# Decode attention on one core: one head of four batches a step, 8 KB of keys per partition, Q used as transposed

## The chip, the cores and the metric

One core of a Trainium2 chip. The metric is the device time of one execution, in microseconds (us). Each run has a state: "fast", or "slow" where it lies over 1.5% above the fastest of the same kernel, and "unknown" where there is only one.

Engine names in the profile: PE is the matmul engine, PEld its weight load, DVE the vector engine, ACT the scalar engine, POOL the general-purpose engine, SP the engine that issues the DMAs (SPq is its queue). L848 means line 848 of that kernel's source. Line numbers shift between kernels.

## The reference

Two attention layers, A and B, whose outputs are joined along the last axis. Both have 16 batches, 32 query tokens a batch, a model width of 1024, 32 query heads of 128 and 1024 cached keys. A has 4 key/value heads, each used by 8 query heads; B has 32, one per query head. All data is bf16.

```python
q = transpose((x @ wq).reshape(B, Sq, H, Dh), 0, 2, 1, 3)
scores = einsum("bhqd,bhkd->bhqk", q, k_cache) * (Dh ** -0.5)
p = softmax(scores, axis=-1)
o = einsum("bhqk,bhkd->bhqd", p, v_cache)
return transpose(o, 0, 2, 1, 3).reshape(B, Sq, H * Dh) @ wo
```

B's key cache has 16 x 32 heads of 256 KB (1024 keys x 256 bytes): 134 MB. B's values are as much again, and everything together is 340 MB. Neighbouring heads of one batch lie next to each other in memory; the same head of the next batch lies 32 heads, 8 MiB, further on.

## The kernel before

The kernel is a list of operations with declared reads and writes, ordered by a list scheduler. B runs in 128 steps. A step handles four (batch, head) pairs of 32 queries, so that the 128 rows of a score tile are full. The four pairs are two neighbouring heads of two batches.

Keys arrive with the key index on the partitions. Four 32-partition quadrants of the PE array are used as separate small arrays (32x32 tiles, 402 ns a score matmul); a DVE transpose (on pairs of bf16, 1223 ns for 128x1024 of them) puts the head dimension on the 32 partitions of a quadrant.

```python
# B's step: heads h0, h0+1 of batches b0, b0+1
ksrc = pb["k"][q.b0:q.b0 + 2, q.h0:q.h0 + 2].rearrange("t hh (p s) d -> (hh p) t (s d)", s=16)
pr.add("sp", lambda e: e.dma_start(KB_sb[:, sl, :, :], ksrc), ...)            # 1 MB, two pieces of 4 KB a partition
for t_ in range(2):
    vsrc = pb["v"][q.b0 + t_, q.h0:q.h0 + 2].rearrange("hh (p c) d -> p hh c d", c=NCH)
    pr.add("sp", lambda e, ...: e.dma_start(VB_sb[:, sl, t_, :, :, :], vsrc), ...)   # 512 KB, 2 KB pieces
# ... (cut)
# transposes of the keys, two a step
pr.add("dve", lambda e: e.transpose(KBt_sb[:, sl, t_, :].bitcast(F32), KB_sb[:, rs, t_, :].bitcast(F32)), ...)
```

A head's keys fill 64 partitions, two quadrants, so the queries of one batch are needed in all four quadrants. After the transpose of the projected queries (`QBt`) they lie in one quadrant only. Small matmuls with an identity, the "shuffle", copy them, and ACT moves the result to `QR`:

```python
for rg in range(4):
    last = e.matmul(QSH[0][32 * rg:32 * rg + 32, 0:2 * Dh]..., ident[32 * a:32 * a + 32, 32 * a:32 * a + 32], rhs,
                    start=True, stop=True, tile_position=(32 * a, 32 * rg))
# ... (cut)
evac(QR[:, gp, a, :, :], QSH[0][:, 0:2 * Dh]..., eng="act", ...)
```

The rest of a step: scores into PSUM, one exp over 128x1024 (1029 ns) with the row sum as a by-product (200 ns for its read), a PE transpose of the probabilities, their product with V, and the scaling. A's steps, projections and output products are put between by the scheduler. Two key slots and three value slots are the buffers.

## Time and profile before

| | before |
|---|---|
| time, median of 3 runs | 914.93 us (910.07 to 921.08) |
| the one issuing queue, share of 16 DMA engines | 97.6% |
| PE busy | 783.4 us, 86% |
| DVE, ACT busy | 57%, 51% |

The first lines come from the page of the kernel before: busy time per engine as a share of the span, then one digit per fortieth of the span (the busy tenths of the 16 DMA engines), then the packets that the DMA engines moved, counted cumulatively by size, and the queue's share of the 16 engines' time.

```profile
span 911.5 us, 28186 instructions
...
PE 783.4 (86%) x12610; PEld 432.9 (47%) x12610; DVE 519.3 (57%) x891; ACT 462.1 (51%) x853; POOL 67.9 (7%) x76
...
DMA  9789899999999999999999999999999999899995
...
DMA packets 151934, 341.64 MB, mean 375 GB/s; under 512 B 10496, under 2 KB 26880, under 8 KB 151808
q1 hardware_dynamic: 151808, 339.78, 97.6%
```

The DMA engines have almost no free time in any slice; PE is next. The following line is from the table by stretches (window, length, busy us and count for PE, PEld, DVE, ACT and POOL, then granted PE clock, DMA share, GB/s). In the middle of the kernel the share is a little over 1, because packets overlap somewhat (17 or more were in flight during 385 us of the span, my own count).

```profile
300.00:323.00 23.00, 20.13 (x354) 10.64 (x341) 12.53 (x22) 10.26 (x21) 2.08 (x2) 0.93 1.04 409
```

Three groups of the kernel before, with busy us, mean ns of one, and idle time ahead of them with what ended it: the key transpose; the shuffle (split by shape, since its tile is shared with other matmuls) and the ACT copies behind it.

```profile
L848 DVE STREAM_TRANSPOSE KBt_sb<-KB_sb 128x1024 f32<-128x1024 f32 x256 | 306.6, 1223 | 46.3 <-DMA KB_sb<-in_B_k_cache_dram 22.6
...
L694 PE MATMUL ps_pj<-QBt,ident 32*32 32x256 bf16 x512 | 43.9, 287 | 17.5 <-ACT QR L588 10.0 <-DVE acc L748 2.6 <-DVE Qtok L590 1.5
...
L588 ACT CAST QR<-ps_pj 128x256 bf16<-128x256 f32 x128 | 48.5, 379 | 46.0 <-PE ps_pj L694 43.3
```

The transposes wait only 22.6 us in all for the key DMA. Last, the DMA issues (count, KB each, us from issue to landing):

```profile
KB_sb<-in_B_k_cache_dram SPq DMA_DIRECT2D x128, 1024.0 KB, 8.2
VB_sb<-in_B_v_cache_dram SPq DMA_DIRECT2D x256, 512.0 KB, 8.9
```

The single packet records of the trace give the price of a packet on one engine. This is my own count, not a view of the profile:

```
before: size   packets   mean ns   median ns
1 KB           16384      49.4      46
2 KB           92160      85.2      84
4 KB           32768     167.3     159        (all of B's keys)
8 KB              32     351.7     309        (instruction fetches)
```

### The profile page before, as it was taken

To read this page: it belongs to the slowest core of one execution; us is meant where nothing else is said; L and a number is where in the kernel's file an instruction comes from. 1 tells how busy PE (TensorE), PEld (TensorE's weight loads), DVE (VectorE), ACT (ScalarE), POOL (GpSimd) and SP (SyncE) were. 2 spreads that over 40 slices of the span, in tenths; PEclk is the share of its full clock that TensorE was granted. 3 is DMA by queue.
4 is the path that set the end of the run, shared out by engine and by line. 5 is a ranking of instruction groups with operands and counts; after the bars stand their busy time and mean duration, and the time that the engine had idled before them with its cause. 6 is when DMAs were issued, how large, how long until landed. Compare 5 with 4: busy or idle time off the path is not lost.

```text
span 911.5 us, 28186 instructions
## 1 busy us (share of the span) xinstructions
PE 783.4 (86%) x12610; PEld 432.9 (47%) x12610; DVE 519.3 (57%) x891; ACT 462.1 (51%) x853; POOL 67.9 (7%) x76
## 2 busy tenths in 40 slices
PE   5879999999998899988898789989897888978775
PEld 2325564545554454545454455536453445545332
DVE  1415655466645566555756556666665656666553
ACT  2215665655564455655564555555554544646242
POOL 0000000100110010101010010001010100001000
PEclk7879999999999999999999999999999899989898
DMA  9789899999999999999999999999999999899995
GB/s 333 270 302 370 308 399 361 402 385 390 359 380 409 411 349 400 401 381 392 368 405 403 411 374 390 375 346 397 405 408 399 385 398 403 333 409 397 385 410 190
DMA packets 151934, 341.64 MB, mean 375 GB/s; under 512 B 10496, under 2 KB 26880, under 8 KB 151808
## 3 DMA queue, kind: packets, MB, share of 16 engines
q1 hardware_dynamic: 151808, 339.78, 97.6%
q8 instruction: 101, 1.65, 0.7%
q14 instruction: 25, 0.20, 0.1%
HBM read 337.64 MB, written 2.10 MB: 373 GB/s over the span
## 4 chain that ended last, share of the span: by engine, by line
PE 56%; ACT 14%; DVE 13%; DMA 12%; issue 2%; SPq 2%; POOL 0%; POOLq 0%; DVEq 0%; ACTq 0%
PE ps_pj L735 10%; PE ps_s L887 10%; DVE KBt_sb L848 6%; PE ps_o L971 6%; PE ps_pj L657 6%; PE ps_pt L921 6%; ACT P_sb L907 5%; PE ps_pj L674 5%; PE ps_kt L937 4%; DMA KB_sb<-in_B_k_cache_dram 4%; ACT PTA_sb L901 3%; PE ps_s L865 3%; DMA wq_sb<-in_A_wq_dram 3%; DVE acc L748 3%; PE ps_kt L839 2%
## 5 line engine op out<-in xcount | busy, mean ns | idle before, releaser
L848 DVE STREAM_TRANSPOSE KBt_sb<-KB_sb 128x1024 f32<-128x1024 f32 x256 | 306.6, 1223 | 46.3 <-DMA KB_sb<-in_B_k_cache_dram 22.6
L887 PE MATMUL ps_s<-KBt_sb,QR 32*32 32x512 bf16 x4096 | 167.0, 402 | 13.8 <-ACT P_sb L907 7.4
L901 ACT ACTIVATE PTA_sb<-ps_s 128x1024 bf16<-128x1024 f32 x128 | 131.6, 1029 | 73.1 <-PE ps_s L865 59.9
L907 ACT ACTIVATE P_sb<-ps_s 128x1024 bf16<-128x1024 f32 x128 | 131.7, 1029 | 70.3 <-PE ps_pt L921 36.5
L588 ACT COPY PT_sb<-ps_pt 128x512 f32<-128x512 f32 x128 | 74.9, 585 | 150.6 <-PE ps_o L971 116.5
L822 POOL COPY VAp_sb<-VA_sb 128x1024 bf16<-128x1024 bf16 x64 | 66.6, 1040 | 770.5 <-DMA VA_sb<-in_A_v_cache_dram 667.3
L921 PE MATMUL ps_pt<-id,P_sb 128*128 128x128 f32 x512 | 91.7, 302 | 18.4 <-ACT P_sb L907 16.9
L987 DVE TENSOR_SCALAR OB_sb<-ps_o,rinv_all 128x128 bf16<-128x128 f32 x128 | 44.4, 347 | 108.0 <-PE ps_o L971 107.6
L921 PEld LDWEIGHTS ps_pt<-id,P_sb 128*128 128x128 f32 x512 | 74.2, 208 | 43.2 <-ACT P_sb L907 25.2
L971 PE MATMUL ps_o<-VB_sb,PT_sb 128*32 128x128 bf16 x4096 | 84.9, 224 | 8.4 <-DMA VB_sb<-in_B_v_cache_dram 6.7
L865 PE MATMUL ps_s<-QT_sb,KTA_sb 128*128 128x256 bf16 x512 | 85.3, 275 | 4.2 <-ACT PTA_sb L901 2.2
L735 PE MATMUL ps_pj<-woB_sb,OTB_sb 128*128 128x512 bf16 x256 | 75.4, 391 | 12.9 <-DVE acc L748 5.4
L937 PE MATMUL ps_kt<-VAp_sb,PTA_sb 128*128 128x129 bf16 x1024 | 80.3, 221 | 5.4 <-ACT KTA_sb L588 2.3
L971 PEld LDWEIGHTS ps_o<-VB_sb,PT_sb 128*32 128x32 bf16 x4096 | 60.1, 98 | 52.1 <-issue 38.7
L657 PE MATMUL ps_pj<-xT_sb,wq_sb 128*128 128x512 bf16 x256 | 74.0, 406 | 11.4 <-DMA wq_sb<-in_A_wq_dram 4.2
L887 PEld LDWEIGHTS ps_s<-KBt_sb,QR 32*32 32x32 bf16 x4096 | 49.7, 90 | 67.5 <-issue 19.5
L937 PEld LDWEIGHTS ps_kt<-VAp_sb,PTA_sb 128*128 128x128 bf16 x1024 | 64.9, 98 | 31.2 <-issue 13.4
L674 PE MATMUL ps_pj<-wq_sb,xT_sb 128*128 128x512 bf16 x256 | 71.0, 391 | 4.3 <-ACT QR L588 1.8
L735 PE MATMUL ps_pj<-woA_sb,OTA_sb 128*128 128x512 bf16 x256 | 66.9, 389 | 7.4 <-DVE ost L751 4.7
L588 ACT CAST QR<-ps_pj 128x256 bf16<-128x256 f32 x128 | 48.5, 379 | 46.0 <-PE ps_pj L694 43.3
L748 DVE TENSOR_TENSOR acc<-acc,ps_pj 128x512 f32<-128x512 f32 x64 | 43.5, 680 | 44.6 <-PE ps_pj L735 44.2
L865 PEld LDWEIGHTS ps_s<-QT_sb,KTA_sb 128*128 128x128 bf16 x512 | 44.3, 98 | 32.3 <-ACT PTA_sb L901 5.8
(52 smaller groups left out, 574.0 us busy)
## 6 DMA issues: line engine op xcount, KB each, us to landing
KB_sb<-in_B_k_cache_dram SPq DMA_DIRECT2D x128, 1024.0 KB, 8.2
VB_sb<-in_B_v_cache_dram SPq DMA_DIRECT2D x256, 512.0 KB, 8.9
KA_sb<-in_A_k_cache_dram SPq DMA_DIRECT2D x64, 256.0 KB, 9.5
VA_sb<-in_A_v_cache_dram SPq DMA_DIRECT2D x64, 256.0 KB, 7.7
wq_sb<-in_B_wq_dram SPq DMA_DIRECT2D x32, 256.0 KB, 6.9
wq_sb<-in_A_wq_dram SPq DMA_DIRECT2D x32, 256.0 KB, 8.7
woB_sb<-in_B_wo_dram SPq DMA_DIRECT2D x32, 256.0 KB, 8.4
woA_sb<-in_A_wo_dram SPq DMA_DIRECT2D x32, 256.0 KB, 7.8
```

Source lines behind the costliest of these rows:

```text
L588: pr.add("act", lambda e: e.copy(dst_ap, src_ap), reads=reads, writes=writes, name=name + "@act", wtag=wtag, rtag=rtag)
L657: last = e.matmul(ps_pj[:, 0:tn], wq_sb[:, 0, j, hc * Dh:(hc + 1) * Dh], xT_sb[:, 0, j, t0:t0 + tn], start=(j == 0), stop=(j == DJ - 1))
L674: last = e.matmul(ps_pj[:, 0:CW], xT_sb[:, 1, j, G * P:(G + 1) * P], wq_sb[:, 1, j, :], start=(j == 0), stop=(j == DJ - 1))
L735: last = e.matmul(ps_pj[:, 0:OUTW], OT[:, gp, hh, :], wo_[:, hh, oh * OUTW:(oh + 1) * OUTW], start=(hh == 0), stop=(hh == nh - 1))
L848: pr.add("dve", lambda e: e.transpose(KBt_sb[:, sl, t_, :].bitcast(F32), KB_sb[:, rs, t_, :].bitcast(F32)), reads=[("KB", rs)], writes=[(" ...
L865: last = e.matmul(ps_s[:, sbf, c2, i * 2 * P:(i + 1) * 2 * P], KTA_sb[:, sl, c * P:(c + 1) * P], qt, start=True, stop=True)
L887: last = e.matmul(ps_s[32 * cg:32 * cg + 32, sbf, g2, :].rearrange("p (s j) -> p s j", s=16), lhsT, rhs, start=(fp == 0), stop=(fp == 3), ...
L901: pr.add("act", lambda e: e.activation(dst, src, ACTF.Exp, scale=scale), writes=BK_S[sbf] + [("PTA", q.half)], name="expA", rtag={("Sv", s ...
L907: pr.add("act", lambda e: e.activation(dst, src, ACTF.Exp, scale=scale, accum_out=stat[:, 0:1]), writes=BK_S[sbf] + ["P", "rowsum"], name= ...
L921: last = e.transpose(ps_pt32[:, m * P:(m + 1) * P], p32[:, m:Sk // 2:NPK], id32[:])
L937: last = e.matmul(ps_kt[:, qh * OA0:qh * OA0 + Dh + 1], PTA_sb[:, h, c, qh * P:(qh + 1) * P], VAp_sb[:, sl, 4 * h + c, 0:Dh + 1], start=(h ...
L971: last = e.matmul(ps_o[32 * a:32 * a + 32, 0:Dh], PT_pairs[:, c // 2, 32 * a:32 * a + 32, c % 2], VB_sb[:, kvs, a // 2, a % 2, c, :], star ...
```

## The change

Intent: a step takes one head of four batches instead of two heads of two. Each batch then has its own quadrant, where its transposed queries already lie, so the shuffle and `QR` go. A head's 1024 keys fill 32 partitions with 8 KB each in one piece, so the key packets are twice as large and half as many. The price: exp must be split in two (the two halves of a batch's keys end in different quadrants of the score tile), with two tiny DVE additions for the row sum.

```diff
-                ksrc = pb["k"][q.b0:q.b0 + 2, q.h0:q.h0 + 2].rearrange("t hh (p s) d -> (hh p) t (s d)", s=16)
-                pr.add("sp", lambda e: e.dma_start(KB_sb[:, sl, :, :], ksrc), ...)
+                ksrc = pb["k"][q.b0:q.b0 + 4, q.h].rearrange("a (p s) d -> a p (s d)", s=32)
+                pr.add("sp", lambda e: e.dma_start(KB_sb[:, sl, :, :].rearrange("p i n -> p (i n)"), ksrc), ...)
 ... (V loads: two batches of one head each, same sizes)
-        def qprepB_sh(m_, G, a_list):            # the shuffle and its copies to QR
-            ... (cut)
+        def qprepB(m_, G):                       # only the transpose, into two slots
+            ... (cut)
-                                    lhsT = QR[32 * rg:32 * rg + 32, gp, a, q.hp, o0:o0 + 63:2]
+                        lhsT = QBt[32 * a:32 * a + 32, gp, q.hh * Dh + o0:q.hh * Dh + o0 + 63:2]
 ... (eight 32x32 score matmuls a group as before)
-                pr.add("act", lambda e: e.activation(dst, src, ACTF.Exp, scale=scale, accum_out=stat[:, 0:1]), ...)
+                for g in range(2):
+                    ... (cut: src and dst of half the columns)
+                    pr.add("act", lambda e, ...: e.activation(dst, src, ACTF.Exp, scale=scale, accum_out=st[:, g:g + 1]), ...)
+                for i in range(2):
+                    pr.add("dve", lambda e, ...: e.tensor_tensor(st[o:o + 64, 2:3], st[o:o + 64, 0:1], st[r:r + 64, 1:2], ALU.add), ...)
 ... (the transpose of the probabilities and the V product follow the new placement)
```

The built program shows the key load's source as 4 x 32 x 4096 elements, outermost first. The four batches are 8 MiB apart, so the first two dimensions can't be joined. Before, it was 128 x 2 x 2048.

More of the change, by code (lines that the diff above doesn't have):

```diff
@@ L18 @@
 LAZY_DELAY = 0
-QSH_IN_PJ = True
 A_STEPS_FRAC = 0.92
@@ L26 @@
 PRIO_BONUS = {}
-PE_MODE = {"scoresB": 2, "Qshuf": 2, "PVB": 1}
+PE_MODE = {"scoresB": 2, "PVB": 1}
 MODE_SWITCH = 0.11
@@ L31 @@
     "scoresB": 1.1, "scoresA": 0.45, "PT_trB": 0.50, "PVB": 0.8, "OT_tr": 0.10, "KTA_tr": 0.50,
-    "Qshuf": 0.25, "qprojA": 1.8, "qprojB": 1.8, "oprojA": 1.8, "oprojB": 0.9, "xT_tr": 0.5,
-    "exp": 1.25, "expA": 1.05, "VAp_cp": 1.2, "normA@dve": 0.42, "OT_trA": 0.2, "OT_evA@dve": 0.35, "PT_ev@act": 0.52, "norm@act": 0.46, "OT_ev@act": 0.24, "KTA_ev@act": 0.93, "qA_ev@act": 0.52, "qB_ev@act": 0.52,
-    "QR_ev@act": 0.31, "acc0": 0.52, "xT_ev@act": 0.93, "o_fin@act": 0.52,
+    "qprojA": 1.8, "qprojB": 1.8, "oprojA": 1.8, "oprojB": 0.9, "xT_tr": 0.5,
+    "exp": 0.82, "shift": 0.12, "expA": 1.05, "VAp_cp": 1.2, "normA@dve": 0.42, "OT_trA": 0.2, "OT_evA@dve": 0.35, "PT_ev@act": 0.52, "norm@act": 0.46, "OT_ev@act": 0.24, "KTA_ev@act": 0.93, "qA_ev@act": 0.52, "qB_ev@act": 0.52,
+    "acc0": 0.52, "xT_ev@act": 0.93, "o_fin@act": 0.52,
     "KBt_tr": 1.15, "recip": 0.15, "norm@dve": 0.30, "PT_ev@dve": 0.62, "OT_ev@dve": 0.16, "KTA_ev@dve": 0.62,
     "QBt_tr": 0.35, "acc+": 0.62, "accF": 0.62, "qA_ev@dve": 0.62, "qB_ev@dve": 0.62, "xT_ev@dve": 0.62, "o_fin@dve": 0.62,
-    "QR_ev@dve": 0.35,
     "c0": 0.2, "c1": 0.3,
@@ L531, in build @@
         z32 = sb("z32", [P, P], F32)
-        stat = sb("stat", [P, 4], F32)
+        stat = sb("stat", [P, 2, 4], F32)
         rinv_all = sb("rinv_all", [P, 2 * NIT], F32)
@@ L540, in build @@
         Qtok = sb("Qtok", [P, 2, NG, CW], BF)
-        QBt = sb("QBt", [P, CW], BF)
-        QR = sb("QR", [P, 2, 4, 2, Dh], BF)
+        QBt = sb("QBt", [P, 2, CW], BF)
         woA_sb = sb("woA_sb", [P, HS, D], BF)
@@ L549, in build @@
         KBt_sb = sb("KBt_sb", [P, 2, 2, 16 * Dh], BF)
-        VB_sb = sb("VB_sb", [P, NVB, 2, 2, NCH, Dh], BF)
+        VB_sb = sb("VB_sb", [P, NVB, 4, NCH, Dh], BF)
         KA_sb = sb("KA_sb", [P, 2, NCH, Dh], BF)
@@ L569, in build @@
         BK_KT, BK_PT, BK_O, BK_PJ = ("bank", 4), ("bank", 5), ("bank", 6), ("bank", 7)
-        QSH = (ps_pj, BK_PJ) if QSH_IN_PJ else (ps_kt, BK_KT)
         pr.add("pool", lambda g: g.memset(zeros[:], 0.0), writes=["zeros"], name="c0")
@@ L680, in qprojB @@
                  wtag={("Qtok", m_ % 2, G): m_})
-        def qprepB_tr(m_, G):
-            pr.add("dve", lambda e: e.transpose(QBt[:, :].bitcast(F32), Qtok[:, m_ % 2, G, :].bitcast(F32)),
-                   reads=[("Qtok", m_ % 2, G)], writes=["QBt"], name="QBt_tr", rtag={("Qtok", m_ % 2, G): m_}, wtag={"QBt": (m_, G)})
-        def qprepB_sh(m_, G, a_list):
+        def qprepB(m_, G):
             gp = (m_ * NG + G) % 2
-            for a in a_list:
-                def e_sh(e, a=a):
-                    last = None
-                    for rg in range(4):
-                        e_ = rg // 2
-                        rhs = QBt[32 * a:32 * a + 32, :].rearrange("p (hp e x) -> p e hp x", hp=2, e=2)[:, e_, :, :]
-                        last = e.matmul(QSH[0][32 * rg:32 * rg + 32, 0:2 * Dh].rearrange("p (hp x) -> p hp x", hp=2),
-                                        ident[32 * a:32 * a + 32, 32 * a:32 * a + 32], rhs, start=True, stop=True,
-                                        tile_position=(32 * a, 32 * rg))
-                    return last
-                pr.add("pe", e_sh, reads=["QBt", "ident"], writes=[QSH[1]], name="Qshuf", rtag={"QBt": (m_, G)})
-                evac(QR[:, gp, a, :, :], QSH[0][:, 0:2 * Dh].rearrange("p (hp x) -> p hp x", hp=2), reads=[QSH[1]],
-                     writes=[QSH[1], ("QR", gp, a)], name="QR_ev", eng="act", wtag={("QR", gp, a): (m_, G)})
+            pr.add("dve", lambda e: e.transpose(QBt[:, gp, :].bitcast(F32), Qtok[:, m_ % 2, G, :].bitcast(F32)),
+                   reads=[("Qtok", m_ % 2, G)], writes=[("QBt", gp)], name="QBt_tr", rtag={("Qtok", m_ % 2, G): m_}, wtag={("QBt", gp): (m_, G)})
         def wo_loadA(s_):
@@ L785, in mk_quadB @@
             q.G = (t // 4) % NG
-            jb = t % 4
-            q.bp = jb // 2
-            q.hp = jb % 2
-            q.b0 = 4 * q.G + 2 * q.bp
-            q.h0 = q.m * MS + 2 * q.hp
+            q.hh = t % 4
+            q.b0 = 4 * q.G
+            q.h = q.m * MS + q.hh
             q.kvslot = t % 2
@@ L795, in mk_quadB @@
             q.sbuf = None
-            q.first_of_group = (jb == 0)
-            q.last_of_group = (jb == 3)
+            q.first_of_group = (q.hh == 0)
+            q.last_of_group = (q.hh == 3)
             q.qid = ("B", t)
@@ L811, in st_dmaK @@
                 sl = q.krslot
-                ksrc = pb["k"][q.b0:q.b0 + 2, q.h0:q.h0 + 2].rearrange("t hh (p s) d -> (hh p) t (s d)", s=16)
-                pr.add("sp", lambda e: e.dma_start(KB_sb[:, sl, :, :], ksrc), writes=[("KB", sl)], dma_key=f"kb{sl}", name="kb_dma", dur=4 * Sk * Dh * 2, wtag={("KB", sl): q.kid})
+                ksrc = pb["k"][q.b0:q.b0 + 4, q.h].rearrange("a (p s) d -> a p (s d)", s=32)
+                pr.add("sp", lambda e: e.dma_start(KB_sb[:, sl, :, :].rearrange("p i n -> p (i n)"), ksrc), writes=[("KB", sl)], dma_key=f"kb{sl}", name="kb_dma", dur=4 * Sk * Dh * 2, wtag={("KB", sl): q.kid})
         def st_dmaV(q):
@@ L826, in st_dmaV @@
                 for t_ in range(2):
-                    vsrc = pb["v"][q.b0 + t_, q.h0:q.h0 + 2].rearrange("hh (p c) d -> p hh c d", c=NCH)
-                    pr.add("sp", lambda e, t_=t_, vsrc=vsrc: e.dma_start(VB_sb[:, sl, t_, :, :, :], vsrc), writes=[("VB", sl, t_)],
+                    vsrc = pb["v"][q.b0 + 2 * t_:q.b0 + 2 * t_ + 2, q.h].rearrange("a (p c) d -> p a c d", c=NCH)
+                    pr.add("sp", lambda e, t_=t_, vsrc=vsrc: e.dma_start(VB_sb[:, sl, 2 * t_:2 * t_ + 2, :, :], vsrc), writes=[("VB", sl, t_)],
                            dma_key=f"vb{sl}_{t_}", name="vb_dma", dur=2 * Sk * Dh * 2, wtag={("VB", sl, t_): q.kid})
@@ L872, in st_scores @@
                 gp = (q.m * NG + q.G) % 2
+                kt = KBt_sb[:, sl, :, :].rearrange("p i (s x) -> p (i s) x", s=16).rearrange("p (sh g cl) x -> p g sh cl x", g=2, cl=4)
                 def e_s(e, fp):
                     last = None
-                    if True:
-                        f, pd = fp // 2, fp % 2
-                        o0 = f * 64 + pd
-                        for t_ in range(2):
-                            a = 2 * q.bp + t_
-                            for hh in range(2):
-                                cg = 2 * t_ + hh
-                                for g2 in range(2):
-                                    rg = 2 * hh + g2
-                                    lhsT = QR[32 * rg:32 * rg + 32, gp, a, q.hp, o0:o0 + 63:2]
-                                    rhs = KBt_sb[32 * rg:32 * rg + 32, sl, t_, :].rearrange("p (s x) -> p s x", s=16)[:, :, o0:o0 + 63:2]
-                                    last = e.matmul(ps_s[32 * cg:32 * cg + 32, sbf, g2, :].rearrange("p (s j) -> p s j", s=16), lhsT, rhs,
-                                                    start=(fp == 0), stop=(fp == 3), tile_position=(32 * rg, 32 * cg))
+                    f, pd = fp // 2, fp % 2
+                    o0 = f * 64 + pd
+                    for a in range(4):
+                        lhsT = QBt[32 * a:32 * a + 32, gp, q.hh * Dh + o0:q.hh * Dh + o0 + 63:2]
+                        for g in range(2):
+                            cg = a ^ (2 * g)
+                            last = e.matmul(ps_s[32 * cg:32 * cg + 32, sbf, g, :].rearrange("p (sh cl j) -> p sh cl j", sh=4, cl=4), lhsT,
+                                            kt[32 * a:32 * a + 32, g, :, :, o0:o0 + 63:2],
+                                            start=(fp == 0), stop=(fp == 3), tile_position=(32 * a, 32 * cg))
@@ L889, in e_s @@
                     return last
                 for fp_ in range(4):
-                    pr.add("pe", lambda e, fp_=fp_: e_s(e, fp_), reads=[("QR", gp, 2 * q.bp), ("QR", gp, 2 * q.bp + 1), ("KBt", sl, 0), ("KBt", sl, 1)],
+                    pr.add("pe", lambda e, fp_=fp_: e_s(e, fp_), reads=[("QBt", gp), ("KBt", sl, 0), ("KBt", sl, 1)],
                            writes=BK_S[sbf], name="scoresB", dur=0.275, tag="B%d" % q.t,
-                           rtag={("QR", gp, 2 * q.bp): (q.m, q.G), ("QR", gp, 2 * q.bp + 1): (q.m, q.G), ("KBt", sl, 0): q.kid, ("KBt", sl, 1): q.kid},
+                           rtag={("QBt", gp): (q.m, q.G), ("KBt", sl, 0): q.kid, ("KBt", sl, 1): q.kid},
@@ L904, in st_exp @@
             else:
-                src = ps_s[:, sbf, :, :].rearrange("p g (s j) -> p g j s", s=16)
-                dst = P_sb[:, :].rearrange("p (g j s) -> p g j s", g=2, s=16)
-                pr.add("act", lambda e: e.activation(dst, src, ACTF.Exp, scale=scale, accum_out=stat[:, 0:1]),
-                       writes=BK_S[sbf] + ["P", "rowsum"], name="exp",
-                       rtag={("Sv", sbf): q.qid}, wtag={"P": q.qid, "rowsum": q.qid})
+                st = stat[:, q.t % 2, :]
+                for g in range(2):
+                    src = ps_s[:, sbf, g, :].rearrange("p (sh cl j) -> p j sh cl", sh=4, cl=4)
+                    dst = P_sb[:, :].rearrange("p (j sh g cl) -> p g j sh cl", sh=4, g=2, cl=4)[:, g]
+                    pr.add("act", lambda e, src=src, dst=dst, g=g: e.activation(dst, src, ACTF.Exp, scale=scale, accum_out=st[:, g:g + 1]),
+                           writes=[BK_S[sbf][g], ("P", g), ("rowsum", q.t % 2, g)], name="exp",
+                           rtag={("Sv", sbf): q.qid}, wtag={("P", g): q.qid, ("rowsum", q.t % 2, g): q.qid})
+                for i in range(2):
+                    o, r = 64 * i, 64 * (1 - i)
+                    pr.add("dve", lambda e, o=o, r=r: e.tensor_tensor(st[o:o + 64, 2:3], st[o:o + 64, 0:1], st[r:r + 64, 1:2], ALU.add),
+                           reads=[("rowsum", q.t % 2, g) for g in range(2)], writes=[("total", q.t % 2, i)], name="shift",
+                           rtag={("rowsum", q.t % 2, g): q.qid for g in range(2)}, wtag={("total", q.t % 2, i): q.qid})
         NPK = NCH // 2
@@ L916, in st_ptr, with e_pt @@
             p32 = P_sb[:, :].bitcast(F32)
-            def e_pt(e):
-                last = None
-                for m in range(NPK):
-                    last = e.transpose(ps_pt32[:, m * P:(m + 1) * P], p32[:, m:Sk // 2:NPK], id32[:])
-                return last
-            pr.add("pe", e_pt, reads=["P", "id32"], writes=[BK_PT], name="PT_trB", rtag={"P": q.qid}, wtag={"PTps": q.qid})
+            for g in range(2):
+                def e_pt(e, g=g):
+                    last = None
+                    for m in (2 * g, 2 * g + 1):
+                        last = e.transpose(ps_pt32[:, m * P:(m + 1) * P], p32[:, m:Sk // 2:NPK], id32[:])
+                    return last
+                pr.add("pe", e_pt, reads=[("P", g), "id32"], writes=[BK_PT], name="PT_trB", dur=0.25, rtag={("P", g): q.qid}, wtag={"PTps": q.qid})
         def st_pev(q, eng="act"):
@@ L970, in e_pv @@
                     for a in range(4):
-                        last = e.matmul(ps_o[32 * a:32 * a + 32, 0:Dh], PT_pairs[:, c // 2, 32 * a:32 * a + 32, c % 2], VB_sb[:, kvs, a // 2, a % 2, c, :],
+                        last = e.matmul(ps_o[32 * a:32 * a + 32, 0:Dh], PT_pairs[:, c // 2, 32 * (a ^ (c // 4 * 2)):32 * (a ^ (c // 4 * 2)) + 32, c % 2], VB_sb[:, kvs, a, c, :],
                                         start=(c == 0), stop=(c == NCH - 1), tile_position=(0, 32 * a))
@@ L978, in st_recip @@
         def st_recip(q):
-            pr.add("dve", lambda e: e.reciprocal(q.rinv, stat[:, 0:1]), reads=["rowsum"], writes=["rinv", ("rinv_all", 1)], name="recip",
-                   rtag={"rowsum": q.qid}, wtag={"rinv": q.qid})
+            pr.add("dve", lambda e: e.reciprocal(q.rinv, stat[:, q.t % 2, 2:3]), reads=[("total", q.t % 2, i) for i in range(2)], writes=["rinv", ("rinv_all", 1)], name="recip",
+                   rtag={("total", q.t % 2, i): q.qid for i in range(2)}, wtag={"rinv": q.qid})
         def st_norm(q, eng="act"):
@@ L994, in st_otr @@
             gp = (q.m * NG + q.G) % 2
-            dst = OTB_sb[:, gp, 2 * q.hp:2 * q.hp + 2, 64 * q.bp:64 * q.bp + 64].rearrange("p hh (t q) -> p t hh q", t=2)
-            evac(dst, ot_ps.rearrange("p (t hh q) -> p t hh q", t=2, hh=2), reads=[BK_O],
-                 writes=[BK_O] + [("OT", 1, gp, h_) for h_ in (2 * q.hp, 2 * q.hp + 1)], name="OT_ev", eng=eng,
+            evac(OTB_sb[:, gp, q.hh, :], ot_ps, reads=[BK_O], writes=[BK_O, ("OT", 1, gp, q.hh)], name="OT_ev", eng=eng,
                  rtag={"OTps": q.qid}, wtag={("OTv", 1, gp): (q.m, q.G)} if q.last_of_group else None)
@@ L1069, in build @@
         qprojB(0, 0)
-        qprepB_tr(0, 0)
-        qprepB_sh(0, 0, [0, 1, 2, 3])
+        qprepB(0, 0)
         for hh in range(MS):
@@ L1117, in build @@
             tn = t + (4 - t % 4)
-            if tn < NIT:
-                qn = quadsB[tn]
-                if t % 4 == 0:
-                    qprepB_tr(qn.m, qn.G)
-                qprepB_sh(qn.m, qn.G, [t % 4])
+            if tn < NIT and t % 4 == 0:
+                qprepB(quadsB[tn].m, quadsB[tn].G)
             if qB.m + 1 < NMSB:
```

## The prediction

> **What bounds the kernel now.** The DMA engines. The page gives them a 97.6% busy share for the one issuing queue and 375 GB/s over the span; in the table by stretches it is 1.01 to 1.04 at 387 to 410 GB/s (packets overlap a little). PE is second: 783 us busy (86%), 20.1 of 23 us in those stretches. DVE is at 57%, ACT at 51%. The queue's own waits (220 us of key loads waiting for the transposes that free a slot) hide behind 8 to 9 us of loads in flight. The packet records show the price of a packet on one engine: median 46 ns for 1 KB, 84 for 2 KB, 159 for 4 KB: 9 ns plus 37.5 per KB. The only 8 KB packets (32 instruction fetches) took 309.
>
> **What the change means to do.** K in 8 KB instead of 4 KB packets: 16384 fewer fixed costs, about 9 us over 16 engines. PE loses the 512 shuffle matmuls (43.9 us, and 17.5 us idle before them). ACT loses 128 casts to QR (48.5 us) but two half-width exps replace one: 256 x (about 590 + 200 for the sum's read) = 202 us against 157 us now, so ACT stays even. DVE gains 256 tiny additions at about 150 ns, 38 us. Scores still use eight 32x32 tiles a group: about the same (167 us). That alone: 890 to 905 us.
>
> **What I think decides it.** The built program shows the key load's source as 4 x 32 x 4096 elements (outermost: four batches, 8 MiB apart), against 128 x 2 x 2048 before. [...] Every load in this trace has 128 outermost, so no run here shows it yet. If it holds, all 134 MB of B's keys go through 4 of 16 engines: 16384/4 = 4096 packets x 309 ns = 1266 us on each. These four also carry their sixteenth of everything else: 491 us (2 KB packets) + 51 (1 KB) + 6 (semaphores). Together 1814 us; divided by 1.03 for overlap, 1760; plus start, tail and some starvation, about 1820 us. All of it is on the critical path: V, A's loads and weights queue behind the keys on those four engines.
>
> **Predicted:** 1820 us, 8 in 10 between 1720 and 1960. Faster by over 2%: 0.09; within 2%: 0.04; slower: 0.87.
>
> **What would show it.** Mean DMA share about 0.45 to 0.5 and about 187 GB/s in the 40 slices; 16384 packets of 8 KB at about 309 ns; a key load takes about 15 us or more from issue to landing (8.2 now); DVE's key transposes wait for the key DMA for hundreds of us (22.6 now) and lead the waits; PE about 720 to 740 us busy, near 40% of the span; the shuffle gone; scores about 400 ns a matmul; exp about 590 ns.
>
> **What would make it wrong.** The queue spreading by the destination's 128 partitions alone: then 890 to 905 us. Or the lowering re-cuts the source. Four quadrants 8 MiB apart colliding in memory: then slower than 309 ns a packet and over 1900 us.

I expected four engines, as many as the source has outer items; it was not shown by any trace or run at that point, and "it" is that expectation, a guess. 1266 + 491 + 51 + 6 = 1814 us, divided by 1.03 it is 1760, with 60 for start, tail and starvation 1820.

## The result, and the profile after

| | before | after |
|---|---|---|
| time, median of 4 runs each | 914.26 us | 2073.9 us (2060.95 to 2100.04) |
| ratio of fast runs | | 2.262 (95%: 2.242 to 2.282) |

Ratios here and below are the mean time of one kernel's fast runs over that of the other's of the same rounds, so they are not quite the ratio of the medians quoted. One of the four runs after (2100.04) was slow and isn't in the ratio.

The changed kernel takes more than twice the time. From its page, the lines that answer to those of before, with the granted PE clock in tenths added:

```profile
span 2071.4 us, 27525 instructions
...
PE 967.8 (47%) x12098; PEld 522.6 (25%) x12098; DVE 568.3 (27%) x1147; ACT 449.9 (22%) x981; POOL 67.9 (3%) x76
...
PEclk9777777677776666767676677677676666677665
DMA  5654555454555555555555645555555555554554
...
DMA packets 134013, 341.58 MB, mean 165 GB/s; under 512 B 8960, under 2 KB 25344, under 8 KB 117504
q1 hardware_dynamic: 133888, 339.77, 53.2%
```

The same 340 MB now move with the DMA engines half busy: neither the DMA engines as a group nor any other engine is full. That is the sign of a limit inside the group. Over the same stretch as before:

```profile
300.00:323.00 23.00, 13.98 (x175) 7.10 (x173) 4.50 (x9) 6.97 (x16) 1.04 (x1) 0.74 0.51 157
```

The chain that ended last (shares of the span by engine) shows what everything waits for; five groups of instructions follow, then the largest of the DVE and PE waits for a DMA (total us, times, longest), then the DMA issues.

```profile
DMA 76%; SPq 11%; DVE 6%; PE 5%; issue 2%; POOL 0%; ACT 0%; POOLq 0%; DVEq 0%
```

```profile
L827 DVE STREAM_TRANSPOSE KBt_sb<-KB_sb 128x1024 f32<-128x1024 f32 x256 | 306.6, 1227 | 1010.3 <-DMA KB_sb<-in_B_k_cache_dram 974.2
L955 PE MATMUL ps_o<-VB_sb,PT_sb 128*32 128x128 bf16 x4096 | 116.5, 272 | 460.2 <-DMA VB_sb<-in_B_v_cache_dram 274.5
...
L863 PE MATMUL ps_s<-KBt_sb,QBt 32*32 32x512 bf16 x4096 | 176.3, 436 | 31.5 <-DVE KBt_sb L827 25.5
...
L886 ACT ACTIVATE P_sb<-ps_s 128x512 bf16<-128x512 f32 x256 | 151.4, 597 | 94.2 <-PE ps_pt L905 50.7
...
L653 PE MATMUL ps_pj<-xT_sb,wq_sb 128*128 128x512 bf16 x256 | 91.4, 489 | 90.6 <-DMA wq_sb<-in_A_wq_dram 46.6
```

```profile
DVE KBt_sb L827 <- DMA KB_sb<-in_B_k_cache_dram: 974.2, 121, 12.8
...
PE ps_o L955 <- DMA VB_sb<-in_B_v_cache_dram: 274.5, 40, 12.5
```

```profile
KB_sb<-in_B_k_cache_dram SPq DMA_DIRECT2D x128, 1024.0 KB
VB_sb<-in_B_v_cache_dram SPq DMA_DIRECT2D x256, 512.0 KB, 22.7
```

DVE waits 974.2 us for keys, where it waited 22.6 us. The V loads, whose own form did not change, take 22.7 us to land instead of 8.9. DVE's and ACT's instructions cost what they did (1227 ns for the transpose, 1223 before); those of PE have grown, and with them PE's busy time, at a granted clock of 0.705 over the span against 0.962 before.

Two things point at four engines. First, the count of packets under 512 bytes, nearly all of them 4-byte semaphore writes, fell from 10496 to 8960. That is 1536 = 128 x 12: each of the 128 key loads sends 12 semaphore packets fewer. Secondly, the number of packets in flight: exactly four during 936 us of the span and five during 181 us.

The semaphores agree. The 4-byte packets are as many as the updates of DMA semaphores in the trace of the kernel before (10496 of each); after the change there are 8960 packets and 9088 updates, one more for each of the 128 key loads. Each of the two key semaphores has 320 updates for its 64 loads, five a load, where it had 1024 before, 16 a load. One key load in the trace, issued at 987.9 us, shows it: its semaphore is updated once at 988.9 us (the trace shows the update, not its size), then at 1006.9, 1007.0, 1010.2 and 1014.8 us. This is probably why the page gives no landing time for the key load.

What did not agree is the price of a packet. Again from the packet records:

```
after: size    packets   mean ns   median ns   highest 5% from
2 KB           92160     115.7      84          192
8 KB           16420     368.3     309          618
```

(36 of the 8 KB packets are instruction fetches.) The median of the 8 KB packets is the 309 ns that the prediction used. The mean is 368.3, and 618 is twice 309.

### The profile page after: what moved, and what is told of

It is laid out like the page before. It is cut to its first block, busy times and chain, and to the rows that moved or that the text cites. A ratio compares the mean times of both kernels' runs of the same rounds, so it can differ in the third digit from the quotient of the medians.

```text
span 2071.4 us, 27525 instructions
## 1 busy us (share of the span) xinstructions
PE 967.8 (47%) x12098; PEld 522.6 (25%) x12098; DVE 568.3 (27%) x1147; ACT 449.9 (22%) x981; POOL 67.9 (3%) x76
## 2 busy tenths in 40 slices
DMA packets 134013, 341.58 MB, mean 165 GB/s; under 512 B 8960, under 2 KB 25344, under 8 KB 117504
## 4 chain that ended last, share of the span: by engine, by line
DMA 76%; SPq 11%; DVE 6%; PE 5%; issue 2%; POOL 0%; ACT 0%; POOLq 0%; DVEq 0%
DMA KB_sb<-in_B_k_cache_dram 49%; DMA VB_sb<-in_B_v_cache_dram 14%; DMA KA_sb<-in_A_k_cache_dram 7%; DVE KBt_sb L827 5%; SPq L807 4%; DMA VA_sb<-in_A_v_cache_dram 4%; SPq L635 2%; SPq L792 2%; DMA wq_sb<-in_A_wq_dram 1%; SPq L787 1%; DMA wq_sb<-in_B_wq_dram 1%; SPq L689 1%; PE ps_pj L653 1%; PE ps_o L955 1%; PE ps_s L863 1%
## 5 line engine op out<-in xcount | busy, mean ns | idle before, releaser
L827 DVE STREAM_TRANSPOSE KBt_sb<-KB_sb 128x1024 f32<-128x1024 f32 x256 | 306.6, 1227 | 1010.3 <-DMA KB_sb<-in_B_k_cache_dram 974.2
L955 PE MATMUL ps_o<-VB_sb,PT_sb 128*32 128x128 bf16 x4096 | 116.5, 272 | 460.2 <-DMA VB_sb<-in_B_v_cache_dram 274.5
L863 PE MATMUL ps_s<-KBt_sb,QBt 32*32 32x512 bf16 x4096 | 176.3, 436 | 31.5 <-DVE KBt_sb L827 25.5
L886 ACT ACTIVATE P_sb<-ps_s 128x512 bf16<-128x512 f32 x256 | 151.4, 597 | 94.2 <-PE ps_pt L905 50.7
L818 PE MATMUL ps_kt<-ident,KA_sb 128*128 128x128 bf16 x512 | 62.3, 297 | 210.1 <-DMA KA_sb<-in_A_k_cache_dram 196.2
L921 PE MATMUL ps_kt<-VAp_sb,PTA_sb 128*128 128x129 bf16 x1024 | 107.4, 264 | 47.2 <-POOL VAp_sb L801 31.8
L801 POOL COPY VAp_sb<-VA_sb 128x1024 bf16<-128x1024 bf16 x64 | 66.6, 1040 | 1897.8 <-DMA VA_sb<-in_A_v_cache_dram 1865.3
L905 PE MATMUL ps_pt<-id,P_sb 128*128 128x128 f32 x512 | 122.9, 351 | 4.5 <-ACT PT_sb L584 1.6
L921 PEld LDWEIGHTS ps_kt<-VAp_sb,PTA_sb 128*128 128x128 bf16 x1024 | 91.9, 123 | 81.0 <-POOL VAp_sb L801 39.0
L818 PEld LDWEIGHTS ps_kt<-ident,KA_sb 128*128 128x128 bf16 x512 | 47.7, 135 | 232.7 <-DMA KA_sb<-in_A_k_cache_dram 211.8
L584 ACT COPY KTA_sb<-ps_kt 128x1024 bf16<-128x1024 bf16 x31 | 31.4, 1012 | 233.0 <-PE ps_kt L818 233.0
L863 PEld LDWEIGHTS ps_s<-KBt_sb,QBt 32*32 32x32 bf16 x4096 | 49.2, 93 | 106.3 <-issue 39.8
## 6 DMA issues: line engine op xcount, KB each, us to landing
VB_sb<-in_B_v_cache_dram SPq DMA_DIRECT2D x256, 512.0 KB, 22.7
```

The lines of the kernel that those rows point to most:

```text
L584: pr.add("act", lambda e: e.copy(dst_ap, src_ap), reads=reads, writes=writes, name=name + "@act", wtag=wtag, rtag=rtag)
L818: last = e.transpose(ps_ktb[:, c * P:(c + 1) * P], KA_sb[:, sl, c, :], ident[:])
L863: last = e.matmul(ps_s[32 * cg:32 * cg + 32, sbf, g, :].rearrange("p (sh cl j) -> p sh cl j", sh=4, cl=4), lhsT, kt[32 * a:32 * a + 32, g, ...
L886: pr.add("act", lambda e, src=src, dst=dst, g=g: e.activation(dst, src, ACTF.Exp, scale=scale, accum_out=st[:, g:g + 1]), writes=[BK_S[sbf ...
L905: last = e.transpose(ps_pt32[:, m * P:(m + 1) * P], p32[:, m:Sk // 2:NPK], id32[:])
L921: last = e.matmul(ps_kt[:, qh * OA0:qh * OA0 + Dh + 1], PTA_sb[:, h, c, qh * P:(qh + 1) * P], VAp_sb[:, sl, 4 * h + c, 0:Dh + 1], start=(h ...
```

## The experiments

Unless said otherwise, an experiment is the changed kernel with the edit shown. Some read the wrong keys. The comparison with the reference on the chip passes for them all the same: with inputs of 0.1 the scores are so near zero that the softmax is nearly flat, whichever keys are used. So "correct" says little about keys here; which versions read the right ones is told below by their construction.

### 1. The source alone: four neighbouring heads (e1_contig, and e1b_contig beside run 6)

The same bytes, packets, layout and program, but the four outer items are neighbouring heads of one batch, so that the source is one unbroken 128 x 4096. Wrong keys.

```diff
-                ksrc = pb["k"][q.b0:q.b0 + 4, q.h].rearrange("a (p s) d -> a p (s d)", s=32)
+                ksrc = pb["k"][q.b0 + q.hh, q.m * MS:q.m * MS + 4].rearrange("a (p s) d -> (a p) (s d)", s=32)
```

> The changed kernel with one edit: the source of B's key load is four neighbouring heads of one batch, one unbroken 1 MB, so that its slowest dimension is 128 rows of 8 KB. The result is wrong on purpose; amounts, packet size (8 KB), destination and all computing are the change's own. If the four outer items of the source alone cause the slowdown, this takes 880 to 910 us, with 16 semaphore packets a key load again, 8 KB packets at about 309 ns and a DMA share near 0.97. If instead the 8 KB packets, the split exp or the adjacent score matmuls cost time, it stays above 950 us.

Measured: 895.53 us (891.39 to 897.53) against 919.84 before on the same chip, ratio 0.9741 (0.9675 to 0.9807). The page of this run:

```profile
PE 737.0 (83%) x11952; PEld 423.7 (47%) x12098; DVE 561.1 (63%) x1147; ACT 446.5 (50%) x981; POOL 68.1 (8%) x76
...
DMA  9799999999999999999999999999999999999994
...
DMA packets 135549, 341.59 MB, mean 383 GB/s; under 512 B 10496, under 2 KB 26880, under 8 KB 119040
q1 hardware_dynamic: 135424, 339.78, 98.4%
...
KB_sb<-in_B_k_cache_dram SPq DMA_DIRECT2D x128, 1024.0 KB, 8.3
```

One line of addresses makes the difference between 2074 and 896 us. The semaphore packets are back at 10496, the load lands in 8.3 us, and the 8 KB packets cost 326 ns in the mean. Everything else of the change, new exp, additions, score tiles and all, is in this run too; so none of it costs anything that matters, and the intended change gains 2.6% here (2.2% when repeated beside run 6). It is clearly faster than before, but whether by over 2% is not settled: the interval crosses that line.

### 2. Four loads, one per batch (e2_split4)

The obvious mend: each batch's keys as a load of its own, 32 partitions, with 32 as the slowest dimension. That all 16 engines take part was my expectation; the count of small packets below shows it. The keys are right.

```diff
+                for a in [0, 1, 2, 3]:
+                    ksrc = pb["k"][q.b0 + a, q.h].rearrange("(p s) d -> p (s d)", s=32)      # shortened
+                    ... e.dma_start(KB_sb[32 * a:32 * a + 32, sl, :, :].rearrange("p i n -> p (i n)"), ksrc) ...
```

> The changed kernel with its key load cut into four loads, one a batch, each 32 partitions of 8 KB; each side's slowest dimension is then 32 and all 16 engines take part; the result is right. If only the number of engines counts: 885 to 930 us and 8 KB packets at about 309 ns. [...] 8 KB packets at about 600 ns, about 300 us more than that, so 1150 to 1250 us.

The condition cut before the second range was a theory of how the destination slows the engines, which no run shows; its 600 ns, about twice 309, was my estimate on that theory.

Measured: 1375.88 us (one run), dearer than either expectation. From its page:

```profile
DMA  9999899989999999998999989899999999999995
...
DMA packets 141697, 341.65 MB, mean 249 GB/s; under 512 B 16640, under 2 KB 33024, under 8 KB 125184
...
KB_sb<-in_B_k_cache_dram SPq DMA_DIRECT2D x512, 256.0 KB, 13.7
```

All 16 engines are busy now (16640 small packets = 10496 + 384 x 16, so each of the 384 added loads uses 16), and still the kernel takes half as long again as before. The packets themselves became slow: 8 KB cost 579 ns in the mean, with a median of 598.

### 3. The pitch in memory (e4_pitch)

Still four outer items and four engines, but heads of one batch, 768 KB apart instead of 8 MiB. This asks whether 8 MiB collides in memory, which the prediction named as a danger. Wrong keys.

```diff
-                ksrc = pb["k"][q.b0:q.b0 + 4, q.h].rearrange("a (p s) d -> a p (s d)", s=32)
+                ksrc = pb["k"][q.b0 + q.hh, (q.t % 22):(q.t % 22) + 10:3].rearrange("a (p s) d -> a p (s d)", s=32)
```

> The changed kernel, still four outer items in the source, but 768 KB apart (every third head of one batch) instead of 8 MiB. The result is wrong on purpose. It asks why the slow kernel took 2074 us and not the 1820 us predicted. If the 8 MiB spacing of the four key streams makes them collide in HBM: the mean of the 8 KB packets falls from 368 ns to about 315 ns and the time to 1780 to 1880 us. [...] nothing changes, 2030 to 2120 us, mean 8 KB packet 350 to 385 ns.

The condition cut before the second range named a place at the destination where the packets might meet, which was not shown; the range is for a pitch that does not matter.

Measured: 2072.87 us (one run), 8 KB packets 368.9 ns in the mean, against 2073.9 us and 368.3 ns. So 8 MiB is no worse than 768 KB. Both are multiples of a head's 256 KB; a pitch that is not was not tried.

### 4. Two loads of two outer items (e3_two)

Two batches a load: two engines, if the engines are again as many as the outer items, as they were with four. The keys are right.

```diff
+                for a in range(2):
+                    ksrc = pb["k"][q.b0 + 2 * a:q.b0 + 2 * a + 2, q.h].rearrange("a (p s) d -> a p (s d)", s=32)
+                    ... e.dma_start(KB_sb[64 * a:64 * a + 64, sl, :, :].rearrange("p i n -> p (i n)"), ksrc) ...
```

> The changed kernel with its key load cut in two loads of two batches (64 partitions each), so that the source's slowest dimension is 2. [...] 8192 key packets of 8 KB each at 305 to 309 ns are 2500 us, with the sixteenth of all else 3000 us, with collisions up to 3700 us; 4 data-carrying semaphore packets a key megabyte (2 a load). If the queue spread these over 16 engines or over four as before, it would take about 900 or 2070 us.

The 305 ns is my estimate (the shortest 8 KB packet in the traces of the kernel before and of the changed kernel took 307).

Measured: 3288.49 us (one run). There are 8960 small packets = 10496 - 128 x 16 + 256 x 2, two for each of the 256 key loads, and exactly two packets are in flight during 2170 us. With two outer items two engines work, as four did with four.

### 5. Four heads of one batch, by column-tiled projections (v2_heads)

A right version of run 1: a step takes four heads of one batch, one per quadrant, so that the keys are one unbroken megabyte. The queries of the four heads must then reach four quadrants; here the projection does it with 32-column tiles.

```diff
-                        last = e.matmul(ps_pj[:, 0:CW], xT_sb[:, 1, j, G * P:(G + 1) * P], wq_sb[:, 1, j, :], ...)
+                        for a in range(4):
+                            last = e.matmul(ps_pj[32 * a:32 * a + 32, bb * Dh:(bb + 1) * Dh], xT_sb[:, 1, j, t0:t0 + Sq],
+                                            wq_sb[:, 1, j, a * Dh:(a + 1) * Dh], ..., tile_position=(0, 32 * a))
```

> A right kernel with the change's aim and an unbroken key load: a step takes four heads of one batch, a head per partition quadrant; the projection of B's queries writes a head to each quadrant (128 matmuls of 32 columns by 128 instead of 8 of 128 by 512), so no shuffle is needed. Key load: 128 rows of 8 KB in one stride, 16 engines. Expected 880 to 910 us, 0.96 to 0.985 of before. If the projection's 128 small matmuls (about 20 ns each, as for B's PV product, so 2.6 against 1.6 us, 32 times: +30 us of PE) matter more than the removed shuffle (44 us busy, 17 us idle), it is at or above before.

Measured: 974.84 us (962.37 to 982.03), ratio 1.057 (1.0505 to 1.0636): a miss. Three of its six runs were slow; the ratio uses the other three (962.37 to 972.39). The profiled run is a slow one (977.28 us, granted clock 0.936). In it PE is busy for 781.9 us instead of 737.0 in run 1, in 15828 matmuls instead of 11952, and PE has 55% of the chain that ended last, 44% in run 1. So PE's added work is the likely cause; no run takes it apart.

### 6. The packet size alone (e6_4k beside e1b_contig)

Run 1 with the key load of the kernel before: two 4 KB pieces a partition instead of one of 8 KB. Wrong keys.

```diff
+                hp, bp = q.hh % 2, q.hh // 2
+                ksrc = pb["k"][q.b0 + 2 * bp:q.b0 + 2 * bp + 2, q.m * MS + 2 * hp:q.m * MS + 2 * hp + 2].rearrange("t hh (p s) d -> (hh p) t (s d)", s=16)
```

> The changed kernel with the key load of before (128 rows, two pieces of 4 KB each; keys of wrong heads and batches, so wrong on purpose). It parts the gain of the whole load with 8 KB packets from that of the dropped shuffle. If packets of 8 KB save what they cost less (2 x 159 - 309 = 9 ns, 16384 times, over 16 engines: 9 us), this is 5 to 13 us above the run with the unbroken 8 KB load of the same call. If they save nothing, within 3 us of it.

> The kernel with the unbroken 1 MB key load again (wrong on purpose), beside the 4 KB one on one chip: 0.967 to 0.981 of before, as in the first call.

Measured, same rounds on one chip: 894.2 us with 4 KB (ratio to before 0.9756, 0.9715 to 0.9798), 897.0 us with 8 KB (0.9775, 0.9727 to 0.9824; one of its six runs was slow and isn't in the ratio). The expected 9 us do not appear: a miss. Larger packets gained nothing measurable, and the gain over before belongs to the rest of the change. PE's busy time fell from 783.4 to 740.2 us in this run, as much as the 43.9 us of the shuffle. That the gain comes from this is the likely reading; the parts of the rest were not run one by one.

### 7. Eight loads of 16 partitions (e5_split8)

If run 2 is slow because of the number of loads, eight should be slower by that; if because a load goes to few neighbouring partitions, 16 of them should be worse than 32.

```diff
+                for a in [0, 1, 2, 3, 4, 5, 6, 7]:
+                    ... e.dma_start(KB_sb[16 * a:16 * a + 16, sl, :, :]..., ksrc) ...          # half of one batch's keys each
```

> The changed kernel with its key load in eight loads of 16 partitions each; the result is right[...]. [...] 8 KB packets near 4 x 309 = 1240 ns[...], a step 8 x 1.24 + 4.2 = 14 us, so 1800 to 2300 us. If it was the number of loads in the run with four: 1380 to 1500 us. If neither: about 900 us.

The factor of four in 4 x 309 = 1240 ns was my guess, and the range of 1800 to 2300 us rests on it.

Measured: 1442.72 us (one run), 8 KB packets 665 ns in the mean. That lies in the range of the theory that I held to be wrong, the number of loads, so this run alone decides nothing. The forecast of 1240 ns was nearly twice too high, though run 8 speaks for the destination in run 2: with 16 neighbouring partitions instead of 32 the packet rose only from 579 to 665 ns, and the time by 67 us. Why so little was not looked into.

### 8. Four loads again, to every fourth partition (e7_step4)

Run 2 with another destination: load a goes to partitions a, a+4, a+8 and so on, instead of 32 neighbours. Same number of loads, same bytes, same source, same engines. The keys land in the wrong quadrants.

```diff
-                    ... e.dma_start(KB_sb[w_ * a:w_ * a + w_, sl, :, :].rearrange("p i n -> p (i n)"), ksrc)
+                    ... e.dma_start(KB_sb[a:P:4, sl, :, :].rearrange("p i n -> p (i n)"), ksrc)
```

> The run with four loads of 32 partitions (1376 us, 8 KB packets at 579 ns), with one edit: load a goes to partitions a, a + 4, a + 8 and so on instead of 32 neighbours. Sources, number of loads and of engines are the same[...]. Keys land in wrong rows, so it is wrong on purpose. [...] 8 KB packets near 310 to 340 ns and 885 to 930 us. If the number of loads or the memory side is the cause: 1340 to 1410 us and 550 to 600 ns.

The first range is for the case that the destination's partitions are the cause.

Measured: 933.37 us (one run) instead of 1375.88.

```profile
DMA  8799999999999999899999999999999999999993
...
DMA packets 141698, 341.66 MB, mean 367 GB/s; under 512 B 16640, under 2 KB 33024, under 8 KB 125184
...
KB_sb<-in_B_k_cache_dram SPq DMA_DIRECT2D x512, 256.0 KB, 6.5
```

The packet counts are the same to a packet (141698 and 141697), the time from issue to landing is 6.5 us instead of 13.7, and an 8 KB packet costs 334 ns in the mean instead of 579. So the destination's partitions cause run 2's loss, and the larger number of loads costs at most some 40 us (933.37 against 893.68 us for run 10 on the same chip). In run 2 the median 8 KB packet took 598 ns, near twice the 309 of the changed kernel. How 32 neighbouring partitions slow the packets is not shown.

### 9. Eight outer items (e8_eight)

Half of the keys of eight heads of one batch, so that eight engines should serve a load. Wrong keys.

```diff
+                ksrc = pb["k"][q.b0 + q.hh, (q.t % 10):(q.t % 10) + 22:3, 0:512].rearrange("a (p s) d -> a p (s d)", s=32)
```

> The changed kernel with eight outer items in the source of its one key load (half the keys of eight heads, wrong on purpose). [...] eight engines, so 8 semaphore packets a key load (2 engines gave 3288 us, four 2074, sixteen 895). 2048 key packets on each: at 305 ns 625 + 504 = 1130 us; [...] (370 to 580 ns) 1260 to 1700 us. If the queue used four engines whenever it can't use 16: 2070 us.

The second range takes 8 KB packets at the 370 to 580 ns that other runs measured.

Measured: 1813.56 us (one run), above both ranges for eight engines: a miss. Eight engines it is: 9472 small packets = 10496 - 128 x 8, and exactly eight packets in flight during 503 us. But the mean 8 KB packet costs 546 ns, so twice the engines win little. Even the 8 KB packets with no 1 or 2 KB packet beside them cost 430 ns here (counted as under run 11, where four key engines have 318), so eight key engines do slow each other. Why was not tested.

### 10. The right version: four heads of one batch, queries projected transposed (v3_heads)

As in run 5 a step takes four heads of one batch, whose keys are one unbroken megabyte. Now the projection gives the queries with the head dimension on the partitions: columns of the weights in steps of four are the stationary operand, which puts 32 dimensions of each of the four heads into the four quadrants at once. No transpose of the queries, no shuffle.

```diff
-                        last = e.matmul(ps_pj[:, 0:CW], xT_sb[:, 1, j, G * P:(G + 1) * P], wq_sb[:, 1, j, :], ...)
+                        lhsT = wq_sb[:, 1, j, fp:CW:4]
+                        last = e.matmul(ps_pj[:, 0:NTOK], lhsT, xT_sb[:, 1, j, :], ...)
-                ksrc = pb["k"][q.b0:q.b0 + 4, q.h].rearrange("a (p s) d -> a p (s d)", s=32)
+                ksrc = pb["k"][q.b, q.h0:q.h0 + 4].rearrange("a (p s) d -> (a p) (s d)", s=32)
-            pr.add("dve", lambda e: e.transpose(KBt_sb[:, sl, t_, :].bitcast(F32), KB_sb[:, rs, t_, :].bitcast(F32)), ...)
+            pr.add("dve", lambda e: e.transpose(KBt_sb[...]...rearrange("p (s u i) -> p s u i", u=2, i=32),
+                                                KB_sb[...]...rearrange("p (s i u) -> p s u i", i=32, u=2)), ...)
-                        lhsT = QBt[32 * a:32 * a + 32, gp, q.hh * Dh + o0:q.hh * Dh + o0 + 63:2]
+                        lhsT = QB_sb[32 * a:32 * a + 32, q.m % 2, fp, q.b * Sq:(q.b + 1) * Sq]
```

> A right kernel: a step takes four heads of one batch, a head per quadrant, key load of 128 rows of 8 KB in one stride. The queries are projected as transposed, 128 columns of the weights in steps of four as stationary operand, so that the result already stands by head and by a quarter of the head's width: 128 by 512 matmuls as before, no shuffle and no transpose of Q. The DVE transposes of the keys read their pairs in steps of two. Expected 875 to 900 us, 0.955 to 0.98 of before; PE busy about 735 us, DVE 14 us below the run with the unbroken load (547). If the stepped reads slow the transposes (now 1223 ns) or the stepped weight loads the projections, it is above 900.

Measured: 893.68 us (887.66 to 897.58) against 913.91 before, ratio 0.9767 (0.9721 to 0.9812). It beats both kernels (2.3% below the kernel before; as in run 1 the interval crosses 2%). DVE is busy 9 us less than in run 1, where 14 were expected. The keys are right in a simulation with inputs of unit scale, where the keys do matter: its output was as close to the reference as that of the kernel before, and that of run 1 was not.

```profile
PE 739.7 (83%) x11960; PEld 426.9 (48%) x12098; DVE 552.1 (62%) x1115; ACT 447.5 (50%) x981; POOL 67.9 (8%) x76
...
DMA packets 135549, 341.59 MB, mean 384 GB/s; under 512 B 10496, under 2 KB 26880, under 8 KB 119040
```

384 GB/s against 375, with PE at 739.7 us busy. It is no faster than run 1, whose addresses it has, so the queries' new path costs nothing visible.

### 11. Four outer items to eight neighbouring partitions each (e10_apart)

What made the 8 KB packet 368 ns dear in the changed kernel, with only four engines on the keys? One answer is that they meet each other at the destination. Here the load is cut into four, so that an outer item goes to eight neighbouring partitions instead of 32. That the four engines then keep apart was my guess. Wrong keys.

```diff
+                for a in [0, 1, 2, 3]:
+                    ksrc = pb["k"][q.b0 + q.hh, (q.t % 22):(q.t % 22) + 10:3, 256 * a:256 * a + 256].rearrange("h (p s) d -> h p (s d)", s=32)
+                    ... e.dma_start(KB_sb[32 * a:32 * a + 32, sl, :, :].rearrange("p i n -> p (i n)"), ksrc) ...
```

> As the changed kernel still four engines per key load (source of four outer items, here a quarter of the keys of four heads of one batch, three heads apart; wrong keys on purpose), but the load is cut into four of 32 partitions, so that each outer item goes to 8 neighbouring partitions[...]. Nothing else differs but the number of loads, 512 for 128, which the run with steps of four bounds at 38 us. [...] mean near 309 to 330 ns, 1800 to 1930 us. [...] mean 355 to 370 ns, 2040 to 2120 us. Semaphore packets: 10496 - 128 x 16 + 512 x 4 = 10496 if four engines serve each load.

The first range is for key engines that meet each other at the destination, the second for any other cause.

Measured: 2146.55 us (one run), 8 KB packets 372.0 ns in the mean, 10496 small packets. The time is above both expected ranges, the packet price just above the upper one. So this other placing made the packets no cheaper (368.3 ns before it). That speaks against the answer only if the four engines do keep apart here, which is not shown. (The time is 73 us above the changed kernel's, more than run 8 allows for four times as many loads. The queue that issues the loads has 22% of the chain that ended last, 11% in the changed kernel; more was not looked into.)

The packet records of the changed kernel, sorted by how many 1 KB and 2 KB packets (V, A's keys and values, weights) were in flight beside each 8 KB packet, in the mean over its duration, show when they are dear. My own count:

```
changed kernel: small packets beside it    8 KB packets   mean ns   share over 550 ns
none                                        6127          317.9      1%
up to 2                                     3233          351.1      7%
2 to 6                                      2144          373.7     14%
6 to 10                                     1156          419.9     24%
10 to 13                                    2589          436.2     27%
over 13                                     1171          467.9     34%
```

Alone, four key engines pay 318 ns, so even in the changed kernel they hardly slow each other. Beside 10 or more small packets (V loads, mostly) they pay 436 to 468. The excess of all 8 KB packets over 309 adds up to 243 us on each of the four, 161 of it in the last three rows. (e10_apart gives the same picture: 317.2 alone, 446.1 at 10 to 13 and 502.6 over 13.) Full traffic as such is not dear: the same sorting of run 1 gives 312.5 ns beside 10 to 13 small packets. Why the key packets of run 1 are not slowed is not shown. One place in the trace of the changed kernel, with a single 8 KB packet in flight, looks as if a key packet and one other engine slow each other: from 1012.1 us that packet took 613 ns, and meanwhile the 2 KB packets of what looks like one engine took 161, 156 and 176 ns, nearly all others 84.

But this can't be the whole answer. If each key packet slowed only one other engine, three key packets in flight would go with three slowed engines. Counted over the whole trace, of some 13 packets of 2 KB in flight beside three 8 KB packets, 7.9 at a time were slow (over 126 ns, one and a half times 84), and 10.3 in e10_apart; beside no 8 KB packet at all 2.4 of 15.5 were, and in run 1 beside three 0.2. So key and V loads in flight together slow each other well beyond one partner each. Whether that comes from the destination or from the memory side (the two batches of a V load are 8 MiB apart in all of these runs, in run 1 too) is open: for run 2 the loss through the destination is shown by run 8 (933 us against 1376); for the changed kernel no run removes the slowdown.

## Why the prediction was right or wrong

The direction and the mechanism that decides it, four engines for all keys, were right. The time was wrong: 1820 us with a range to 1960, measured 2073.9.

- "Four of 16 engines": right. Shown by the 12 missing semaphore packets per load, by four packets in flight, and by runs 1, 4 and 9 (16, 2 and 8 engines: 896, 3288 and 1814 us).
- "4096 packets x 309 ns = 1266 us on each": this is the step that failed, a term of the sum that was mis-sized. It measured 4096 x 368.3 ns = 1509 us, 243 us more. The 309 ns was the median of 32 instruction fetches, the only 8 KB packets of the kernel before; their mean was already 351.7, and a sum needs the mean. Run 1, with all 16 engines on the keys, has a median of 309 and a mean of 326: even at that price the term would be 1335 us, 69 more than predicted. In the changed kernel most of the excess, 161 of 243 us, lies with 8 KB packets that had more than six small ones beside them (run 11): alone an 8 KB packet cost 318 ns, beside 10 and more small ones 436 to 468. The prediction counted the packets of the four engines and took each at an undisturbed price. What makes the two kinds of load slow each other stays open.
- With 1509 for 1266 the prediction's own sum gives (1509 + 491 + 51 + 6) / 1.03 + 60 = 2057 us, within 17 us of the result. Part of that closeness may be luck: the mean 2 KB packet rose too, from 85.2 to 115.7 ns. The records don't name the engine; if the four key engines had their even share of that rise, 491 would be 666 us and the sum 2229. The fit needs the rise to lie mostly on the other twelve.
- "Four quadrants 8 MiB apart colliding in memory: then over 1900 us": the time went there, but not because of the 8 MiB: run 3, with 768 KB, took the same time.
- DMA share 0.45 to 0.5 and 187 GB/s: measured 0.532 and 165 GB/s. Same cause: the same bytes, held longer by the packets.
- "A key load takes about 15 us or more": about 19 to 27 us for the one load read above. DVE's waits for keys (974.2 us) lead DVE's waits: right. They come second in the whole list, after POOL's 1865.3 us for A's values, idle time of an engine that works for 3% of the span.
- PE 720 to 740 us busy: wrong, 967.8 us. Run 1 has 737.0 us with nearly the same matmuls, so the extra is the slower PE: a projection matmul took 489 ns instead of 406, a V product 272 instead of 224. The granted clock was 0.705 with PE busy for 47% of the span, against 0.984 at 83% in run 1; what lowered it no run takes apart. The chain of waits gives PE 5%, so this cost little. In step with it, scores took 436 ns (about 400 predicted).
- exp at about 590 ns: 597 measured. The shuffle gone: right.
- "That alone: 890 to 905 us" for the change without the four-engine load: run 1 measured 895.53. But the 9 us credited to larger packets did not appear (run 6).

## What to carry to other kernels

Look at the outermost dimension of a DMA's source as it is built, not at its bytes: where two, four or eight items there could not be joined, as few engines did the work (3288, 2074 and 1814 us, against 896 with 16 engines), and a share of busy DMA engines well under 1 (0.532 in the changed kernel) with everything waiting for one load was the sign. Then look at which partitions each load writes: cutting the load so that all 16 engines take part was only half a mend while each piece landed in 32 neighbouring partitions (1376 us, where the same pieces spread over all partitions took 933). And take the price of a packet from its mean beside the traffic it will meet, not from a median of a few undisturbed ones. The cheapest mend here was to choose the four items of a step so that they lie next to each other in memory (893.68 us), after finding a way to bring the queries there.
